# Moving one block's gate work behind the last transposes, and a 1/sqrt chain ahead of a put-off subtraction, in the z stage of an attention and gMLP kernel

## The chip, the cores and the metric

The kernel runs on one core of one Trainium2 chip. The metric is the device time of one execution in microseconds. Before the change it is 1726.86 us, the median of three runs (1726.46 to 1728.48).

## What is computed

Two pre-norm residual layers on `x` of 2048 x 512, in float32:

```
x = A_x
h  = x + attention(layernorm(x))            # 32 heads of 16, full softmax
# gMLP on layernorm(h):
z  = gelu(layernorm(h) @ w_in)              # 512 -> 2 x 688
z1 = z[:, :688]
z2 = layernorm(z[:, 688:])
g  = w_sp @ z2 + b_sp[:, None]              # mixes the 2048 rows
h2 = h + (z1 * g) @ w_out
```

Products that must be exact enough for float32 are made from two float16 parts of each factor (high part, and the difference "low part"), three matmuls each (`mm3`, lines 106 to 109).

## The kernel before, in words

The kernel has three large stages, each written out in an explicit order that the engines keep: attention (up to about 1294 us in the profile), the **z stage** (lines 1237 to 1280, from there to 1455 us), and the **final stage** (from line 1425 on), which multiplies by `w_sp` and `w_out`.

The z stage takes the 2048 rows in 16 blocks of 128, in the order `h_rows` = 0, 1, 8, 9, 2, 10, 3, 11, ..., 7, 15. Iteration `k` of its loop handles block `row[k]`; so iteration 12 is block 6, iteration 13 block 14, iteration 14 block 7 and iteration 15, the last, block 15. The work of an iteration, in the order of the code:

- `make_h` (740 to 752) for the block two iterations ahead (`new`): 12 matmuls on TensorE, then on VectorE the sum with `x` (749) and its statistics (752). The last two iterations have no `new`.
- `split_o` (731 to 738) for the block three ahead: ScalarE makes the high part (735), VectorE the low part (738).
- `make_z(sb, 1, 0)`: 12 matmuls and a gelu on ScalarE (1190) for the first half of the second part of z. `make_z(sb, 1, 1)`, `(0, 0)` and `(0, 1)` follow further down. The tile `z1` of a block is made by the first two, `z0` by the last two; `z0` has one buffer, `z1` four.
- `turn` (1170 to 1177) for the next block: four transposes on TensorE (1175) of the normalised `hn`, then ScalarE copies them out as float16 (`hT`, line 98) and VectorE makes the low part (104). The next iteration's matmuls need both. It stands behind the first `make_z`, in iteration 14 alone behind the second.
- the put-off difference: `subs.pop()(nc.vector)` makes the low part of one gate operand (`b21`, line 1195) that the iteration before left over. Blocks 8 to 14 leave one.
- the **1/sqrt chain of h**: `scale_h` (754 to 757, with `rstd_of`, 111 to 132) and `minus_mean` (764 to 767), ten small VectorE instructions from the variance of h to `nb`, the last input of `hn`.
- `bn_stats` of z on VectorE (1262).
- `hn` on ScalarE (1268), for the block two ahead; TensorE transposes it in the next iteration.
- `gate_z` (1203 to 1235), the **gate work**: a store of `z0` to device memory from ScalarE's queue (1207); VectorE's 1/sqrt chain of z (1209 on), ending in another `nb` (766); the normalisation on ScalarE (1212); and the operands of the final stage in `T`: sums and differences of quarters of z, each with a high part (1194) and a low part (1195), mostly on GpSimd (1218, 1228, 1231, 1234). A block under 8 gives `b11` and `t1`; a block from 8 on gives `t2`, `b22`, `t3`, `b21` and `n4`. The last block has some of these on VectorE and ScalarE.

Each engine executes its own instructions in the order of the code. The final stage begins on TensorE with `product(A, "b11")` (1445), which takes `b11` of the blocks 0 to 7 in turn, then `t1` (1454), `t2` (1463), `b22` (1465), `t3` (1470), `b21` (1475) and `n4` (1485); its weights `raw_w` come by DMA (1430, 1432) and are measured on VectorE (1322) before TensorE's matmul in `measure_w` (1328).

Of the kernel before, what the change touches and what calls it, by code (L numbers as in the profile page):

```python
# [27 lines left out]
NB = S // P  # L28
# [31 lines left out]
def block_kernel(ctx: ExitStack, tc: tile.TileContext, x, wqkv, wo, w_in, w_sp4, b_sp, w_out, out):  # L60
# [7 lines left out]
    nc = tc.nc  # L68
# [26 lines left out]
    def split(hi, lo, src, eh=None, el=None):  # L95

        if eh == "act":
            nc.scalar.activation(hi, src, AF.Copy)  # L98
        elif eh == "pool":
            nc.gpsimd.tensor_copy(hi, src)  # L100
        else:
            nc.vector.tensor_copy(hi, src)
        back = hi if hi.dtype == F16 else hi.bitcast(F32)
        (nc.gpsimd if el == "pool" else nc.vector).tensor_sub(lo, src, back)  # L104

    def mm3(ps, lh, ll, rh, rl, first, last, **kw):
        nc.tensor.matmul(ps, lh, rh, start=first, stop=False, **kw)  # L107
        nc.tensor.matmul(ps, lh, rl, start=False, stop=False, **kw)  # L108
        nc.tensor.matmul(ps, ll, rh, start=False, stop=last, **kw)  # L109

    def rstd_of(pool, var, n, between=lambda: None, up=1.0):

        hv = pool.tile([P, n], F32, name=f"rs_v{n}")
        nc.vector.tensor_scalar(hv, var, EPS, 0.5 / up ** 2, op0=ALU.add, op1=ALU.mult)
        r = pool.tile([P, n], F32, name=f"rs_r{n}")
        nc.vector.tensor_scalar(r.bitcast(I32), hv.bitcast(I32), -0.5, GUESS,
                                op0=ALU.mult, op1=ALU.add)
        t = pool.tile([P, n], F32, name=f"rs_t{n}")
        for i in range(3):
            if i == 1:  # L120
                between()

            if n == 1:
                nc.vector.tensor_scalar(t, r, r, hv, op0=ALU.mult, op1=ALU.mult)  # L124
                u = pool.tile([P, 1], F32, name="rs_u", bufs=6)
                nc.vector.tensor_scalar(u, t, 1.5, r, op0=ALU.subtract, op1=ALU.mult)  # L126
                r = u
            else:
                nc.vector.tensor_mul(t, r, r)
                nc.vector.tensor_mul(t, t, hv)  # L130
                nc.vector.scalar_tensor_tensor(r, t, 1.5, r, op0=ALU.subtract, op1=ALU.mult)
        return r
# [626 lines left out]
    def new_hn(sb):  # L759
        mv, rs = scale_h(sb)  # L760
        hns[sb] = e2.tile([P, D], F32, name="hn", bufs=3)
        nc.vector.tensor_scalar(hns[sb], xrs.pop(sb), mv[:, 0:1], rs, op0=ALU.subtract, op1=ALU.mult)

    def minus_mean(pool, mv, rs):
        nb = pool.tile([P, 1], F32, name="nb")
        nc.vector.tensor_scalar(nb, rs, mv[:, 0:1], -1.0, op0=ALU.mult, op1=ALU.mult)
        return nb
# [396 lines left out]
    with ExitStack() as mid:  # L1164
        m2 = mid.enter_context(tc.tile_pool(name="mid_2", bufs=2))
        zs, zst = {}, {}
        ps = mid.enter_context(tc.tile_pool(name="mid_ps", bufs=5, space=PSUM))
        pt = mid.enter_context(tc.tile_pool(name="mid_pt", bufs=2, space=PSUM))

        def turn(sb):  # L1170

            hn = hns.pop(sb)
            tp = pt.tile([P, DB, P], F32, name="tp")
            for d in range(DB):
                nc.tensor.transpose(tp[:, d, :], hn[:, d * P:(d + 1) * P], ident)
            hTs[sb] = [m2.tile([P, DB, P], F16, name=f"hT{i}") for i in range(2)]
            split(hTs[sb][0], hTs[sb][1], tp, "act")

        def new_z(sb):
            zs[sb] = [m2.tile([P, FH], F32, name=f"z{i}", bufs=1 + 3 * i) for i in range(2)]  # L1180
            zst[sb] = m2.tile([P, 2, 6], F32, name="zst")

        def make_z(sb, i, c):

            hT, f = hTs[sb], slice(i * FH + c * FC, i * FH + (c + 1) * FC)
            acc = ps.tile([P, 512], F32, name="acc")
            for d in range(DB):
                mm3(acc[:, :FC], hT[0][:, d, :], hT[1][:, d, :],
                    wi2[0][:, d, f], wi2[1][:, d, f], d == 0, d == DB - 1)
            nc.scalar.activation(zs[sb][i][:, c * FC:(c + 1) * FC], acc[:, :FC], AF.Gelu_apprx_tanh,  # L1190
                                 scale=gelu_down)

        def parts(name, k, src, eh, el):
            (nc.gpsimd.tensor_copy if eh == "pool" else nc.scalar.copy)(T[name][0][:, k, :], src)
            sub = lambda e: e.tensor_sub(T[name][1][:, k, :], src, T[name][0][:, k, :])
            if el == "later":
                subs.append(sub)
            else:
                sub(nc.gpsimd if el == "pool" else nc.vector)

        subs = []

        def gate_z(sb, meanwhile):

            z = zs.pop(sb)
            rows = slice(sb * P, (sb + 1) * P)
            nc.scalar.dma_start(z_scr[rows, :], z[0])
            mv = m2.tile([P, 2], F32, name="zmv")
            nc.vector.bn_aggr(mv, zst.pop(sb))
            rs = rstd_of(m2, mv[:, 1:2], 1, up=Z2_UP)  # L1210
            nb = minus_mean(m2, mv, rs)
            nc.scalar.activation(z[1], z[1], AF.Identity, bias=nb, scale=rs)
            zs[sb] = z[1]
            meanwhile()
            if sb < HB:
                b1, b2 = z[1][:, :FC], z[1][:, FC:]
                parts("b11", sb, b1, "act", "pool")
                nc.gpsimd.tensor_sub(b1, b2, b1)
                parts("t1", sb, b1, "pool", "pool")
                return  # L1220

            k = sb - HB
            (t1, b12), (b21, b22) = ((t[:, :FC], t[:, FC:]) for t in (zs.pop(k), zs.pop(sb)))
            last = k == HB - 1
            e = nc.vector if last else nc.gpsimd
            el, eh = (None, "act") if last else ("pool", "pool")
            t2 = m2.tile([P, FC], F32, name="t2", bufs=1)
            e.tensor_sub(t2, b22, t1)
            parts("t2", k, t2, eh, el)
            parts("b22", k, b22, "pool" if last else "act", "pool")  # L1230
            nc.gpsimd.tensor_sub(b12, b22, b12)
            parts("t3", k, b12, "pool", "pool")
            parts("b21", k, b21, "pool" if last else "act", "pool" if last else "later")
            nc.gpsimd.tensor_sub(t2, b21, t2)
            parts("n4", k, t2, "pool", "pool")

        row = dict(enumerate(h_rows))
        with tc.manual_schedule(engines={E.PE, E.Activation, E.DVE, E.Pool, E.SP}):
            asked.pop(0)()
            turn(row[0])  # L1240
            new_hn(row[1])
            for k in range(NB):
                sb, new = row[k], row.get(k + 2)
                if new is not None:
                    for _ in make_h(new, ps.tile([P, 512], F32, name="acc")):
                        pass
                if k + 3 < NB:
                    split_o(row[k + 3])
                new_z(sb)
                make_z(sb, 1, 0)  # L1250
                if k + 1 < NB and k != NB - 2:
                    turn(row[k + 1])
                if subs:
                    subs.pop()(nc.vector)
                if new is not None:
                    mv, rs = scale_h(new)
                    nb = minus_mean(e2, mv, rs)
                make_z(sb, 1, 1)
                if k == NB - 2:
                    turn(row[k + 1])  # L1260
                for c in range(2):
                    nc.vector.bn_stats(zst[sb][:, c, :], zs[sb][1][:, c * FC:(c + 1) * FC])
                make_z(sb, 0, 0)
                make_z(sb, 0, 1)
                hTs.pop(sb)
                if new is not None:
                    hns[new] = e2.tile([P, D], F32, name="hn", bufs=3)
                    nc.scalar.activation(hns[new], xrs.pop(new), AF.Identity, bias=nb, scale=rs)
                if k == 1:
                    invert()  # L1270
                if k >= NB - 8:
                    ask()

                def meanwhile():
                    if k + 4 < NB:
                        asked.pop(0)()
                    if k + 5 < NB:
                        asked.append(load_o(row[k + 5]))

                gate_z(sb, meanwhile)  # L1280
    early.close()
    late.close()

# [258 lines left out]
```

## Time and profile before

| what | value |
|---|---|
| median of three runs | 1726.86 us (1726.46 to 1728.48) |
| the profiled execution: its time, its span | 1726.86 us, 1725.1 us |
| busy share of the span | TensorE 99%, VectorE 83%, ScalarE 76%, GpSimd 47% |
| first transposes of the z stage, its last matmul | 1294.60 us, 1455.07 us |
| first matmul of the final stage | 1455.22 us |

PE is TensorE's matmuls, PEld its weight loads, DVE is VectorE, ACT ScalarE, POOL GpSimd, SP the DMA queue of SyncE, ACTq the one of ScalarE. A row of a timeline gives the start in us from the span's start, the duration, the engine and line, the operation with output and input, and in brackets how long the engine sat idle before it and what released it. Matmuls are pipelined: a row of 128x344 shows 0.31 us, though the next one starts 0.146 us later; so the distance of starts tells more than the brackets.

### The profile page before, as it was taken

How to read it: one execution, taken by the hardware profiler on the slowest of the kernel's cores; microseconds unless marked ns; L12 is line 12 of the kernel's file. 1: busy time of each engine (PE TensorE's matmuls, PEld its weight loads, DVE VectorE, ACT ScalarE, POOL GpSimd, SP SyncE). 2: the span in 40 equal slices, each digit the busy share in tenths (PEclk: the TensorE clock that was granted, in tenths of full speed). 3: DMA queues.
4: the chain of work that ended last, by engine and by line, in shares of the span. 5: the costliest groups of instructions: out<-in, count | busy, mean ns of one | idle time of the engine just before them, and what ended most of it. 6: DMA issues, size and time to landing. Idle time of an engine off the chain costs nothing.

```text
span 1725.1 us, 36747 instructions
## 1 busy us (share of the span) xinstructions
PE 1708.8 (99%) x13583; PEld 653.4 (38%) x13583; DVE 1438.4 (83%) x3030; ACT 1318.7 (76%) x2598; POOL 815.5 (47%) x1076
## 2 busy tenths in 40 slices
PE   9999999999999999999999999999999999999999
PEld 4433222222222222222222222222216566666665
DVE  7688999999999999999999999999927886433234
ACT  4334999999999999999999999999994554221111
POOL 1231867776672267687677866400013766110010
PEclk9999999999999999999999999999999999999999
DMA  5534332342231234344345343300124464654540
GB/s 183 162 97 144 101 88 69 100 98 81 75 71 27 60 105 117 113 149 135 103 121 146 115 147 103 80 20 12 45 51 135 136 184 159 228 179 145 170 139 25
DMA packets 183932, 190.51 MB, mean 110 GB/s; under 512 B 65704, under 2 KB 134632, under 8 KB 183752
## 3 DMA queue, kind: packets, MB, share of 16 engines
q1 hardware_dynamic: 181448, 182.53, 36.2%
q10 hardware_dynamic: 2304, 5.64, 0.8%
q8 instruction: 106, 1.74, 0.4%
q14 instruction: 74, 0.61, 0.1%
HBM read 122.10 MB, written 65.93 MB: 109 GB/s over the span
## 4 chain that ended last, share of the span: by engine, by line
PE 76%; DVE 15%; DMA 3%; ACT 2%; issue 2%; POOL 2%; SPq 1%; DVEq 0%; ACTq 0%; POOLq 0%
PE pv L828 26%; PE s L803 17%; PE m L223 9%; DVE mx L228 7%; PE acc L107 4%; PE g L109 4%; PE g L108 4%; PE g L107 4%; PE acc L109 3%; PE acc L108 3%; DVE ab L237 1%; DMA rc<-r_scr 1%; DVE og L838 1%; DVE rs_t L124 1%; DVE rs_u L126 1%
## 5 line engine op out<-in xcount | busy, mean ns | idle before, releaser
L812 ACT ACTIVATE pt<-s 128x512 f32<-128x512 f32 x1968 | 1006.3, 637 | 5.1 <-PE m L223 4.0
L228 DVE TENSOR_REDUCE mx<-m 128x1 f32<-128x512 f32 x1510 | 947.5, 682 | 12.6 <-PE m L223 3.9
L803 PE MATMUL s<-qst,kst 50*128 50x512 f16 x2048 | 604.3, 379 | 0.2
L828 PE MATMUL pv<-pt,vst 128*32 128x256 f32 (+1 forms) x6056 | 598.1, 466 | 4.1 <-DVE og L838 1.3
L223 PE MATMUL m<-kst,qst 48*128 48x512 f16 x1510 | 452.4, 381 | 0.0
L803 PEld LDWEIGHTS <-kst 50*128 50x128 f16 x2048 | 131.9, 94 | 352.1 <-issue 323.7
L828 PEld LDWEIGHTS pv<-pt,vst 128*32 128x32 f32 x6056 | 119.5, 108 | 290.3 <-issue 276.9
L223 PEld LDWEIGHTS <-qst 48*128 48x128 f16 x2048 | 159.2, 93 | 173.7 <-issue 124.3
L223 PE MATMUL m<-uvs,qst 48*128 48x512 f16 x504 | 190.5, 380 | 0.3 <-DVE mx L228 0.3
L245 POOL TENSOR_SCALAR nm<-nm 128x16 f32<-128x16 f32 x32 | 6.6, 206 | 359.7 <-DVE nm L242 359.7
L237 DVE CUSTOM_DVE_ANT_0 ab<-m,ab 128x512 f32<-128x512 f32 x252 | 170.5, 677 | 2.7 <-ACT ab L233 2.7
L233 ACT ACTIVATE ab<-m 128x512 f32<-128x512 f32 x252 | 157.3, 624 | 16.5 <-PE m L223 15.8
L989 POOL TENSOR_TENSOR op<-raw,op 128x512 f16<-128x512 f32 x80 | 92.9, 1161 | 6.0
L1467 POOL TENSOR_TENSOR pr<-pr,z 128x344 f32<-128x344 f32 x8 | 7.3, 912 | 176.9 <-DVE pr L1466 173.0
L912 POOL TENSOR_TENSOR raw<-raw 128x512 f32<-128x512 f32 (+1 forms) x84 | 83.3, 991 | 6.7
L917 POOL TENSOR_TENSOR acc_sp<-acc_sp,raw 128x512 f32<-128x512 f32 x63 | 80.5, 1277 | 4.5
L107 PE MATMUL acc<-wi,hT 128*128 128x344 f16 x256 | 79.1, 309 | 1.4 <-ACT hT L98 1.4
L1362 ACT ACTIVATE pr<-pr,up 128x304 f32<-128x304 f32 (+1 forms) x32 | 17.0, 574 | 81.9 <-DVE up L1316 81.9
L109 PE MATMUL acc<-wi,hT 128*128 128x344 f16 x256 | 79.1, 309 | 0.3 <-DVE hT L104 0.3
L108 PE MATMUL acc<-wi,hT 128*128 128x344 f16 x256 | 79.1, 309 | 0.0
L1408 DVE SCALAR_TENSOR_TENSOR h<-acc,low,h 128x512 f32<-128x512 f32 (+1 forms) x33 | 24.1, 732 | 45.8 <-PE acc L109 32.5
L909 POOL TENSOR_SCALAR raw<-raw 128x512 f32<-128x512 f32 (+1 forms) x88 | 52.3, 594 | 19.5 <-DMA raw<-in_wqkv 12.2
(240 smaller groups left out, 2280.1 us busy)
## 6 DMA issues: line engine op xcount, KB each, us to landing
raw<-in_w_sp SPq DMA_DIRECT2D x128, 256.0 KB
s_scr<-op SPq DMA_DIRECT2D x64, 256.0 KB
op<-s_scr SPq DMA_DIRECT2D x32, 512.0 KB
a_scr<-op SPq DMA_DIRECT2D x48, 256.0 KB
op<-a_scr SPq DMA_DIRECT2D x24, 512.0 KB
o_scr<-og SPq DMA_DIRECT2D x64, 128.0 KB
qst<-q_scr SPq DMA_DIRECT2D x192, 32.0 KB
kst<-k_scr SPq DMA_DIRECT2D x48, 128.0 KB
```

The lines of the kernel that those rows point to most:

```text
L107: nc.tensor.matmul(ps, lh, rh, start=first, stop=False, **kw)
L108: nc.tensor.matmul(ps, lh, rl, start=False, stop=False, **kw)
L109: nc.tensor.matmul(ps, ll, rh, start=False, stop=last, **kw)
L223: nc.tensor.matmul(acc, q[r, p, c], keys[r, p], start=True, stop=True)
L228: nc.vector.reduce_max(at(t, e if t else e - 1), acc, axis=AX.X)
L233: nc.scalar.activation(ab[0], acc, AF.Abs)
L237: nc.vector.tensor_tensor_reduce(ab[0], acc, ab[0], 0.5, LOW, ALU.add, ALU.max, at(0, 0))
L803: nc.tensor.matmul(s, kst[hg % 2][r, p, kb * P:(kb + 1) * P], qst[hg * NQ + qb][r, p, :], start=True, stop=True)
L812: nc.scalar.activation(pts[p, kb][:, t, :], s, AF.Exp, scale=scales_[hg // 2])
L828: nc.tensor.matmul(pv[0][32 * j:32 * j + 32, a:b], vst[hg % 2][:, c:c + 32], pts[j % 2, kb][:, j // 2, a:b], start=kb == 0, stop=kb == NB - 1,
L912: pool.tensor_mul(got[0] if n else acc, got[0], got[0])
L989: chores.append((lambda: pool.tensor_sub(t[0][:, 1], of(), t[0][:, 0]), TT))
```

## The change

It does two things in the loop of the z stage. The gate work of iteration 13 (block 14) isn't issued at the end of that iteration but held in `put_off`, and issued in iteration 14 behind `turn` of the last block. And in every iteration the 1/sqrt chain of h with its `minus_mean` stands ahead of the put-off difference, not behind it.

```diff
-        subs = []
+        subs, put_off = [], []
...
                 make_z(sb, 1, 0)
                 if k + 1 < NB and k != NB - 2:
                     turn(row[k + 1])
-                if subs:
-                    subs.pop()(nc.vector)
                 if new is not None:
                     mv, rs = scale_h(new)
                     nb = minus_mean(e2, mv, rs)
+                if subs:
+                    subs.pop()(nc.vector)
                 make_z(sb, 1, 1)
                 if k == NB - 2:
                     turn(row[k + 1])
+                    put_off.pop()()
...
-                def meanwhile():
+                def meanwhile(k=k):
...
-                gate_z(sb, meanwhile)
+                if k == NB - 3:
+                    put_off.append(lambda sb=sb, then=meanwhile: gate_z(sb, then))
+                else:
+                    gate_z(sb, meanwhile)
```

The number and kind of instructions stay the same. First place, VectorE in iteration 12 (`b21_1` is the low part of block 13's gate operand, `mv` and `nb` begin and end the chain of h, `zst` takes the statistics of z). Before, from the low part of `o` on:

```order
L738 SCALAR_TENSOR_TENSOR o21_22576<-o_22394,fig3_1844,o20_22575 128x512
L104 TENSOR_TENSOR hT1_22602<-tp_22596,hT0_22601 128x512
L1195 TENSOR_TENSOR b21_1_20667<-z1_22433,b21_0_20666 128x344
L756 BN_AGGR mv_22606<-st_22573 128x2
L114 TENSOR_SCALAR rs_v1_22608<-mv_22606 128x1
```

and now, the end of the same stretch:

```order
L126 TENSOR_SCALAR rs_u_22619<-rs_t1_22612,rs_u_22616 128x1
L766 TENSOR_SCALAR nb_22621<-rs_u_22619,mv_22605 128x1
L1195 TENSOR_TENSOR b21_1_20667<-z1_22433,b21_0_20666 128x344
L1263 BN_STATS zst_22581<-z1_22580 128x6 x2
L1209 BN_AGGR zmv_22673<-zst_22581 128x2
```

The difference has moved from ahead of the chain's ten instructions to behind them; it still stands ahead of the statistics of z. It is so in the six iterations 3, 4, 6, 8, 10 and 12. A seventh difference, block 14's, went in iteration 14 and now goes in iteration 15.

Second place, ScalarE from `hn` of the last block on (`z0_22714` and `z1_22715` are block 14's z, `z1_22840` and `z0_22839` block 7's, `hT0` the last block's transposes). Before:

```order
L1268 ACTIVATE hn_22802<-xr_22404,nb_22756,rs_u_22754 128x512
L1207 DMA z_scr_81<-z0_22714 128x688
L1212 ACTIVATE z1_22715<-z1_22715,nb_22823,rs_u_22821 128x688
L1194 CAST b22_0_20668<-z1_22715 128x344
L1194 CAST b21_0_20666<-z1_22715 128x344
L1190 ACTIVATE z1_22840<-acc_22842,fig0_1841 128x344
L1190 ACTIVATE z1_22840<-acc_22857,fig0_1841 128x344
L98 ACTIVATE hT0_22876<-tp_22871 128x512
L1190 ACTIVATE z0_22839<-acc_22882,fig0_1841 128x344
L1190 ACTIVATE z0_22839<-acc_22896,fig0_1841 128x344
```

and now (block 7's tiles are `z1_22807` and `z0_22806`):

```order
L1269 ACTIVATE hn_22802<-xr_22404,nb_22756,rs_u_22754 128x512
L1190 ACTIVATE z1_22807<-acc_22809,fig0_1841 128x344
L1190 ACTIVATE z1_22807<-acc_22823,fig0_1841 128x344
L98 ACTIVATE hT0_22842<-tp_22837 128x512
L1207 DMA z_scr_81<-z0_22714 128x688
L1212 ACTIVATE z1_22715<-z1_22715,nb_22863,rs_u_22861 128x688
L1194 CAST b22_0_20668<-z1_22715 128x344
L1194 CAST b21_0_20666<-z1_22715 128x344
L1190 ACTIVATE z0_22806<-acc_22881,fig0_1841 128x344
L1190 ACTIVATE z0_22806<-acc_22895,fig0_1841 128x344
```

Two gelus and the copy of the last transposes have passed the store, the normalisation and two casts of block 14.

Third place, VectorE at the same point. Before, the end of block 14's chain of z, its put-off difference, and then the low part of the last block's transposes:

```order
L126 TENSOR_SCALAR rs_u_22821<-rs_t1_22813,rs_u_22818 128x1
L766 TENSOR_SCALAR nb_22823<-rs_u_22821,zmv_22807 128x1
L1195 TENSOR_TENSOR b21_1_20667<-z1_22715,b21_0_20666 128x344
L104 TENSOR_TENSOR hT1_22877<-tp_22871,hT0_22876 128x512
L1262 BN_STATS zst_22841<-z1_22840 128x6 x2
```

and now:

```order
L766 TENSOR_SCALAR nb_22756<-rs_u_22754,mv_22740 128x1
L1263 BN_STATS zst_22716<-z1_22715 128x6 x2
L104 TENSOR_TENSOR hT1_22843<-tp_22837,hT0_22842 128x512
L1209 BN_AGGR zmv_22847<-zst_22716 128x2
L114 TENSOR_SCALAR rs_v1_22849<-zmv_22847 128x1
```

The low part `hT1` has passed block 14's whole chain of z and its put-off difference. GpSimd's order stays as it was; the inputs of its part of block 14's gate work come from ScalarE's normalisation, which now stands later.

## The prediction, made before the run

> **What bounds the kernel now.** I read the page first, then TensorE's waits within the z stage, then the timelines of the engines around those waits.
>
> ```profile
> span 1725.1 us, 36747 instructions
> PE 1708.8 (99%) x13583; PEld 653.4 (38%) x13583; DVE 1438.4 (83%) x3030; ACT 1318.7 (76%) x2598; POOL 815.5 (47%) x1076
> ```
>
> TensorE is the bound, so the change is worth what it takes from TensorE's idle time, and a part of it at most. The profiled execution took 1726.86 us, the median of the runs shown; a term found in its trace is subtracted from that time. About 0.2%, 3.5 us, is what a measurement of this kernel can tell from no change.
>
> In the z stage TensorE waits in two kinds of place. The first, TensorE at the start of iteration 15:
>
> ```profile
> 1446.07 0.31 PE L109 MATMUL acc<-wi,hT 128*128 128x344 f16 x1
> 1447.78 0.32 PE L107 MATMUL acc<-wi,hT 128*128 128x344 f16 x1 [1.40 <-ACT hT L98]
> 1447.93 0.31 PE L108 MATMUL acc<-wi,hT 128*128 128x344 f16 x1
> 1448.50 0.32 PE L109 MATMUL acc<-wi,hT 128*128 128x344 f16 x1 [0.26 <-DVE hT L104]
> ```
>
> Matmuls follow each other in 0.146 us. From 1446.07 to 1447.78 is 1.71, so 1.56 are lost; from 1447.93 to 1448.50 another 0.42. The sum is **1.99 us**: TensorE waits for the copies of the last block's transposes, which stand on ScalarE and VectorE behind block 14's gate work.
>
> The second kind is small and repeats: TensorE wants to transpose and `hn` isn't there yet. Its waits, and the turns of iterations 12 and 13:
>
> ```profile
> PE tp L1175 <- ACT hn L1268: 1.6, 5, 0.7
> ...
> 1422.62 0.60 PE L1175 MATMUL tp<-ident,hn 128*128 128x128 f32 x4
> 1423.05 0.31 PE L107 MATMUL acc<-wi,hT 128*128 128x344 f16 x1
> ...
> 1432.50 0.31 PE L109 MATMUL acc<-wi,hT 128*128 128x344 f16 x1
> 1433.03 0.66 PE L1175 MATMUL tp<-ident,hn 128*128 128x128 f32 x4 [0.23 <-ACT hn L1268]
> 1433.53 0.31 PE L107 MATMUL acc<-wi,hT 128*128 128x344 f16 x1
> ```
>
> The turn of iteration 13 starts 0.53 behind the last matmul, not 0.146, and its four transposes take 0.50 and not 0.43: 0.45 lost. The brackets hide 0.16 of each wait; with that added to the 1.6 us, a sixth wait hidden wholly, and 0.07 for slow transposes, the six come to about 2.9 us. They stand in iterations 4, 5, 7, 9, 11 and 13, each behind an iteration with a put-off difference.
>
> **What sets `hn`.** ScalarE over two iterations, and VectorE in iteration 12:
>
> ```profile
> 1415.06 0.96 ACT L1212 ACTIVATE z<-z,nb,rs_u 128x688 f32<-128x688 f32 x1 [2.58 <-DVE nb L766]
> ...
> 1421.22 0.81 ACT L1268 ACTIVATE hn<-xr,nb,rs_u 128x512 f32<-128x512 f32 x1 [1.83 <-DVE nb L766]
> ...
> 1424.61 0.96 ACT L1212 ACTIVATE z<-z,nb,rs_u 128x688 f32<-128x688 f32 x1 [2.58 <-DVE nb L766]
> ...
> 1432.17 0.81 ACT L1268 ACTIVATE hn<-xr,nb,rs_u 128x512 f32<-128x512 f32 x1 [2.85 <-DVE nb L766]
> ...
> 1435.56 0.96 ACT L1212 ACTIVATE z<-z,nb,rs_u 128x688 f32<-128x688 f32 x1 [2.58 <-DVE nb L766]
> ```
>
> ```profile
> 1427.12 0.75 DVE L738 SCALAR_TENSOR_TENSOR o<-o,fig,o 128x512 f16<-128x512 f32 x1 [1.16 <-ACT o L735]
> ...
> 1428.04 0.69 DVE L104 TENSOR_TENSOR hT<-tp,hT 128x512 f16<-128x512 f32 x1 [0.16 <-ACT hT L98]
> 1428.65 1.09 DVE L1195 TENSOR_TENSOR b<-z,b 128x344 f16<-128x344 f32 x1
> 1429.66 0.17 DVE L756 BATCH_NORM_AGGREGATE mv<-st 128x2 f32<-128x6 f32 x1
> ...
> 1432.05 0.93 DVE L1262 BATCH_NORM_STATS2 zst<-z 128x6 f32<-128x344 f32 x2
> ```
>
> VectorE and ScalarE form a closed loop: ScalarE's normalisation (1212) waits for VectorE's `nb`, the high part of `o` (735) stands behind it, VectorE's low part (738) waits for that, and from line 104 on VectorE runs without a gap to the next `nb`. Two turns of this loop take 1435.56 - 1415.06 = 20.50 us. TensorE needs less: from the turn at 1422.62 to that at 1433.03 are 10.41, less the 0.39 lost ahead of it 10.02, or 20.04 for two. **So the small waits come from a slower loop, not from where the chain stands in it.** The difference stays ahead of the statistics (1262), hence in the loop.
>
> **Part 1: the chain of h ahead of the difference (six iterations).** The chain starts at 1428.65 and not 1429.66, so `hn` is 1.01 us earlier in these iterations. In the others it doesn't move: there `hn` ends at 1421.22 + 0.81 = 1422.03 and TensorE takes it at 1422.62. Since a waiting transpose starts about 0.05 behind its `hn` (1432.98 to 1433.03), that is 0.54 of slack. TensorE can gain on the loop only until it eats this: the waits move to the even iterations 6 to 12. By iteration 13 TensorE is about 0.95 us ahead of before. Then two more rows cap it:
>
> ```profile
> 1437.37 0.59 ACT L98 ACTIVATE hT<-tp 128x512 f16<-128x512 f32 x1
> ...
> 1441.11 0.81 ACT L1268 ACTIVATE hn<-xr,nb,rs_u 128x512 f32<-128x512 f32 x1 [1.58 <-DVE nb L766]
> ...
> 1444.50 0.96 ACT L1212 ACTIVATE z<-z,nb,rs_u 128x688 f32<-128x688 f32 x1 [2.58 <-DVE nb L766]
> ```
>
> ```profile
> 1437.99 0.69 DVE L104 TENSOR_TENSOR hT<-tp,hT 128x512 f16<-128x512 f32 x1 [1.09 <-ACT hT L98]
> ...
> 1441.95 0.21 DVE L1209 BATCH_NORM_AGGREGATE zmv<-zst 128x2 f32<-128x12 f32 x1
> ```
>
> ```profile
> 1439.07 0.31 PE L109 MATMUL acc<-wi,hT 128*128 128x344 f16 x1
> ...
> 1442.28 0.60 PE L1175 MATMUL tp<-ident,hn 128*128 128x128 f32 x4
> ```
>
> Iteration 14 has no `make_h`, so TensorE reaches its `hT` at once. The low part is there at 1438.68, which lets the matmul of 1439.07 start at 1438.73, 0.34 earlier; the last `hn` ends at 1441.92, which lets the turn of 1442.28 start at 1441.97, 0.31 earlier. So part 1 is worth **0.3 us** if the loop keeps its pace.
>
> The pace hangs on GpSimd. What ran there beside the difference:
>
> ```profile
> 1428.53 0.83 POOL L1195 TENSOR_TENSOR b<-z,b 128x344 f16<-128x344 f32 x1
> 1429.33 1.18 POOL L1231 TENSOR_TENSOR z<-z,z 128x344 f32<-128x344 f32 x1
> ...
> 1431.13 0.84 POOL L1195 TENSOR_TENSOR t<-z,t 128x344 f16<-128x344 f32 x1
> ...
> 1448.90 0.91 POOL L1231 TENSOR_TENSOR z<-z,z 128x344 f32<-128x344 f32 x1
> ```
>
> ```profile
> 1446.38 0.52 DVE L1195 TENSOR_TENSOR b<-z,b 128x344 f16<-128x344 f32 x1 [1.92 <-ACT b L1194]
> ```
>
> Six of the seven differences take 1.09 and the seventh 0.52: in the six, a GpSimd instruction that began 0.12 earlier (1428.53) runs, the difference ends 0.38 behind its end (1429.36 to 1429.74), and GpSimd's next one takes 1.18 and not 0.91. In its new place the difference starts 1428.65 + 1432.05 - 1429.66 = 1431.04. GpSimd's subtraction of 1431.13 comes 0.27 earlier, as nothing lengthens line 1231 any more: 1430.86. It is under way again, ends at 1431.70, and lets the difference end at 1432.08, against 1432.13 if the old 1.09 were simply moved. So the loop gains 0.05 or 0.06 in each of six iterations, 0.35 at most, and part 1 lies between 0.3 and 0.65. I take 0.5, the middle.
>
> The Trainium skill ("SBUF — State Buffer", section "Who interferes with whom") says that a VectorE instruction with two SBUF inputs and a GpSimd instruction that reads SBUF block each other, and that whichever issues first keeps the other out for its whole length. The 0.52 against 1.09 agrees. By this rule the margin of 0.18 us between GpSimd's start and VectorE's decides: 0.5 for part 1 as above, or the first rival's sum.
>
> **Part 2: block 14's gate work behind the last turn.** With that turn at 1441.97 the copies follow it on engines that are free but for two gelus, and `hT` is complete near 1444.1 (0.66 for the transposes, 0.59 and 0.69 for the copies, with two short steps between). TensorE wants it at 1445.90. The 1.99 us go whole. What is moved is late instead. VectorE's chain of z starts at 1444.04 and not 1441.95, **2.09 later**, and with it the normalisation (1446.59 instead of 1444.50) and GpSimd's part:
>
> ```profile
> 1445.54 0.92 POOL L1228 TENSOR_TENSOR t<-z,z 128x344 f32<-128x344 f32 x1 [5.14 <-ACT z L1212]
> ...
> 1453.54 0.84 POOL L1195 TENSOR_TENSOR b<-z,b 128x344 f16<-128x344 f32 x1
> ```
>
> ```profile
> 1458.43 0.31 PE L108 MATMUL g<-b,op 128*128 128x344 f16 x1
> ```
>
> GpSimd works without a gap from 1445.54 through block 14's part to the low part of block 7's `b11` at 1453.54. Moved by 2.09 this ends at 1456.47. TensorE wants it in the eighth group of the first product, at 1458.43 before, now 1.99 + 0.31 earlier: 1456.13. **A new wait of 0.4 us** (0.34 and a start of 0.05). The next product wants `t1` 24 matmuls or 3.5 us behind that, and GpSimd has `t1` about 2.5 us behind `b11`, so that is covered.
>
> The store of `z0` moves too, and block 7's gelus into the one buffer wait for it:
>
> ```profile
> 1359.80 4.57 DMA z_scr<-z
> ```
>
> Issued near 1443.4, a store of 4.6 us (the chain of waits) has landed at 1448.0; ScalarE gets to the gelu at 1448.4. Block 7's own store goes near 1449.3 and makes ScalarE wait at the last block's `z0`, with only the last normalisation behind it, whose `nb` comes later still. Cost: nothing, as long as a store lands within 5 us. Block 14's `b21` goes to VectorE's iteration 15; the sixth product wants it, over 15 us later. `meanwhile` issues nothing in iteration 13. Behind GpSimd's run stand the memset of the last sixth of `raw_w` and SyncE's two small loads into it, 2.1 later:
>
> ```profile
> 1456.76 0.53 POOL L1429 MEMSET raw_w<- 128x512 f32 x1
> ```
>
> ```profile
> 1463.57 3.65 DVE L1322 TENSOR_REDUCE w<-raw_w 128x1 f32<-128x512 f32 x6 [3.29 <-DMA raw_w<-in_w_out]
> ```
>
> VectorE reads that sixth last, near 1466.5, over 6 us behind the new memset; the other five leave at TensorE's last z matmul and come earlier with it. Cost nothing.
>
> **The sum.** -1.99 - 0.5 + 0.4 = -2.1 us: 1726.86 - 2.1 = **1724.8**. With 0.3 to 0.65 for part 1 and 0.2 to 0.8 for the new wait it is 1724.4 to 1725.4.
>
> **Rivals.** *The difference meets a free port* (12%): if it starts ahead of GpSimd's subtraction it takes 0.52, six iterations are 0.5 shorter, the loop is faster than TensorE and all 2.9 us go: -1.99 - 2.9 + 0.4 = -4.5, 1722.4. Against it stands the 0.18 us by which GpSimd is first, the same in each of six repeats.
>
> *GpSimd holds the tail* (9%): VectorE's seventh difference now falls into GpSimd's run, and each meeting adds 0.27. With more of them, or GpSimd starting later, the wait at `b11` grows one for one; at 2.5 us nothing is left: up to 1726.9.
>
> *GpSimd's queue goes first* (5%): if in the new place the next GpSimd instruction too (line 1234, 0.92) gets ahead of the waiting difference, each of six iterations grows by about 0.9, `hn` of the last turn comes 5.4 later (1447.3, against 1442.28 before, so TensorE loses 5.1), and the time is 1726.86 + 5.1 - 1.99 + 0.4 = 1730.4, slower. It decides from the second instruction on; before, VectorE got in behind the first, six times of six.
>
> *The move shows nothing* (3%): a wait that I don't see takes the 2 us; 1726.9.
>
> **How the numbers follow.** The forecast has 71%. Faster by over 0.2% is the first rival, 0.12; slower the third and a little more, 0.06; the rest is 0.82. The range runs from the first rival, 1722.3, to the second, 1726.9, which leaves the third out.
>
> **What would show it.** No wait at line 107 for `hT` at the start of the last iteration; a wait of about 0.4 at the end of the first product for line 1195 on GpSimd; waits of about 0.4 for `hn` in iterations 6, 8, 10 and 12 instead of 7 to 13; differences of still about 1.05 us. Six differences of 0.52 would make the first rival right; 1.9 the third.

## The result, and the profile after

The changed kernel takes **1724.36 us**, the median of 19 runs (1723.85 to 1725.05); the kernel before 1726.76, the median of 19 (1725.97 to 1728.48). The ratio is 0.9986, 95% interval 0.998 to 0.9993: 2.4 us faster, which is within 0.2%. The profiled execution took 1723.98 us, 2.88 less than the one of before. Page of the changed kernel:

```profile
span 1722.2 us, 36747 instructions
...
PE 1709.8 (99%) x13583; PEld 653.6 (38%) x13583; DVE 1438.1 (84%) x3030; ACT 1318.6 (77%) x2598; POOL 813.6 (47%) x1076
```

TensorE's waits in the z stage and the first product now, and those of its weight loads. A column each: total us, times, longest.

```profile
PE acc L109 <- DVE hT L104: 0.3, 1, 0.3
```

```profile
PEld L745 <- DVE o L738: 1.7, 4, 0.5
PEld tp L1175 <- ACT hn L1269: 1.3, 5, 0.3
PEld L109 <- DVE hT L104: 0.6, 1, 0.6
PEld L109 <- issue: 0.3, 1, 0.3
PEld L107 <- ACT hT L98: 0.3, 1, 0.3
```

The wait of the transposes on `hn` (line 1175, 1.6 us before) and the one on ScalarE's `hT` (line 107, 1.4) are gone from TensorE's list. Its weight loads still show small ones, with a new kind, line 745: the product by `wo` waits for the low part of `o` (738), an output of the same loop. TensorE's timeline at the three places of the forecast, the start of iteration 14, the last turn with the start of iteration 15, and the eighth group of the first product:

```profile
1436.88 0.31 PE L109 MATMUL acc<-wi,hT 128*128 128x344 f16 x1
1437.12 0.32 PE L107 MATMUL acc<-wi,hT 128*128 128x344 f16 x1
1437.28 0.31 PE L108 MATMUL acc<-wi,hT 128*128 128x344 f16 x1
1437.85 0.32 PE L109 MATMUL acc<-wi,hT 128*128 128x344 f16 x1 [0.26 <-DVE hT L104]
...
1441.08 0.66 PE L1175 MATMUL tp<-ident,hn 128*128 128x128 f32 x4
...
1444.92 0.31 PE L109 MATMUL acc<-wi,hT 128*128 128x344 f16 x1
1445.07 0.31 PE L107 MATMUL acc<-wi,hT 128*128 128x344 f16 x1
...
1455.13 0.31 PE L107 MATMUL g<-b,op 128*128 128x344 f16 x1
1455.52 0.31 PE L108 MATMUL g<-b,op 128*128 128x344 f16 x1
```

From 1444.92 to 1445.07 is the plain distance of 0.146: the 1.99 us at the start of iteration 15 are gone whole. At the start of iteration 14 there is a new loss of 0.09 + 0.42 = 0.52 for `hT`, and in the eighth group one of 0.24, since GpSimd's low part of `b11` (1454.63, 0.84 long) ends at 1455.47. It is the last of GpSimd's run behind block 14's normalisation, which starts with the first row:

```profile
1446.60 0.92 POOL L1228 TENSOR_TENSOR t<-z,z 128x344 f32<-128x344 f32 x1 [7.11 <-ACT z L1212]
...
1454.63 0.84 POOL L1195 TENSOR_TENSOR b<-z,b 128x344 f16<-128x344 f32 x1
```

I added up in each trace what TensorE's distances of starts have above the plain ones, from the first z matmul to the end of the first product. In all nine kernels of this study the profiled time is the first z matmul plus that sum plus 423.9 (423.84 to 424.00), so this table is the whole of what differs between them:

| kernel | first z matmul | for `hn` and `o`, iterations up to 13 | start and turn of iteration 14 | start of 15 | `b11` | sum | profiled time |
|---|---|---|---|---|---|---|---|
| before | 1298.06 | 2.93 | 0 | 1.99 | 0 | 4.92 | 1726.86 |
| after | 1298.12 | 1.07 | 0.57 | 0 | 0.24 | 1.88 | 1723.98 |
| chain only | 1299.12 | 0.65 | 0.57 | 2.23 | 0 | 3.45 | 1726.53 |
| put-off only | 1297.89 | 2.38 | 0 | 0 | 0.23 | 2.61 | 1724.35 |
| difference behind z | 1298.03 | 0 | 0 | 0 | 0.23 | 0.23 | 1722.11 |
| difference twice | 1298.67 | 7.35 | 1.71 | 0 | 0.51 | 9.58 | 1732.25 |
| store later | 1298.40 | 0 | 0 | 0.92 | 0 | 0.92 | 1723.21 |
| difference behind z alone | 1297.65 | 0 | 0 | 0 | 0 | 0 | 1721.49 |
| `b11` on VectorE | 1297.92 | 1.59 | 0.57 | 0 | 0 | 2.17 | 1724.03 |

The first column differs by 1.5 us though no kernel differs there: in these nine executions the attention stage ended that unevenly, which can be one part of the spread of the runs.

**The pace of the loop.** ScalarE's normalisation of z, one iteration in two, in the changed kernel:

```profile
1393.81 0.96 ACT L1212 ACTIVATE z<-z,nb,rs_u 128x688 f32<-128x688 f32 x1 [3.53 <-DVE nb L766]
...
1414.23 0.96 ACT L1212 ACTIVATE z<-z,nb,rs_u 128x688 f32<-128x688 f32 x1 [3.52 <-DVE nb L766]
...
1434.66 0.96 ACT L1212 ACTIVATE z<-z,nb,rs_u 128x688 f32<-128x688 f32 x1 [3.52 <-DVE nb L766]
```

Two turns take 20.42 us, 0.08 less than before and still more than TensorE's 20.04. VectorE and GpSimd around the difference in its new place:

```profile
1430.07 0.21 DVE L766 TENSOR_SCALAR nb<-rs_u,mv 128x1 f32<-128x1 f32 x1
1430.20 1.03 DVE L1195 TENSOR_TENSOR b<-z,b 128x344 f16<-128x344 f32 x1
1431.16 0.93 DVE L1263 BATCH_NORM_STATS2 zst<-z 128x6 f32<-128x344 f32 x2
```

```profile
1430.02 0.84 POOL L1195 TENSOR_TENSOR t<-z,t 128x344 f16<-128x344 f32 x1
1430.82 1.21 POOL L1234 TENSOR_TENSOR t<-z,t 128x344 f32<-128x344 f32 x1
```

GpSimd is first by 0.18 us, as the prediction worked out, and the difference takes 1.03, six times of six (1.01 to 1.03).

**Where the loop starts.** The normalisation in iteration 2, before and after, with the store ahead of it:

```profile
1331.31 0.33 ACTq L1207 DMA_DIRECT2D z_scr<-z  x1
1331.68 0.96 ACT L1212 ACTIVATE z<-z,nb,rs_u 128x688 f32<-128x688 f32 x1 [4.69 <-DMA o<-o_scr]
```

```profile
1330.82 0.36 ACTq L1207 DMA_DIRECT2D z_scr<-z  x1
1331.23 0.96 ACT L1212 ACTIVATE z<-z,nb,rs_u 128x688 f32<-128x688 f32 x1 [4.17 <-DMA o<-o_scr]
```

VectorE's `nb` for it, in the kernel before:

```profile
1328.19 0.21 DVE L766 TENSOR_SCALAR nb<-rs_u,zmv 128x1 f32<-128x1 f32 x1
```

It was there at 1328.4. The 3.3 us up to the normalisation are spent on the store: it waits for a load of `o` that SyncE issued from 1323.97 on:

```profile
1323.97 2.81 SPq L721 DMA_DIRECT2D o<-o_scr  x4
```

The order of the code is the same in both kernels here; the 0.45 between them is how late that load landed. Over the eight traces in which the store stands there, the normalisation starts at 1330.82 to 1332.36.

So the 2.9 us between the two profiles are: 0.45 this start of the loop, 0.44 the loop itself (from iteration 2 to 12 its normalisations lie 103.87 us apart before and 103.43 after, 0.07 for each of six differences), 0.3 the slack at the last turn (before, `hn` ended at 1441.92 and the turn started at 1442.28), 1.99 the start of iteration 15, less 0.24 for `b11`. Without the 0.45, which is none of the change's, 2.5, beside 2.4 between the medians.

### The profile page after: what moved, and what is told of

Same layout as the page of the kernel before. It is cut to its first block, busy times and chain, and to the rows that moved or that the text cites. A ratio compares the mean times of both kernels' runs of the same rounds, so it can differ in the third digit from the quotient of the medians.

```text
span 1722.2 us, 36747 instructions
## 1 busy us (share of the span) xinstructions
PE 1709.8 (99%) x13583; PEld 653.6 (38%) x13583; DVE 1438.1 (84%) x3030; ACT 1318.6 (77%) x2598; POOL 813.6 (47%) x1076
## 4 chain that ended last, share of the span: by engine, by line
PE 74%; DVE 14%; DMA 4%; POOL 3%; ACT 2%; SPq 2%; issue 2%; ACTq 0%; DVEq 0%; POOLq 0%
PE pv L828 25%; PE s L803 17%; PE m L223 9%; DVE mx L228 7%; PE g L109 3%; PE g L108 3%; PE g L107 3%; PE acc L107 3%; PE acc L109 3%; PE acc L108 3%; DMA rc<-r_scr 2%; DVE ab L237 1%; DVE og L838 1%; DMA raw<-in_w_sp 1%; DVE rs_t L124 1%
```

## The experiments

My theory after the result: one loop, VectorE's two chains with the difference and ScalarE between them, sets all of TensorE's waits by its length and by its start. Rivals: the waits for `hn` come from where the chain of h stands; the two parts are independent; or other waits take over.

**One part alone.** The first kernel has only the chain of h ahead of the difference:

```diff
-                if subs:
-                    subs.pop()(nc.vector)
                 if new is not None:
                     mv, rs = scale_h(new)
                     nb = minus_mean(e2, mv, rs)
+                if subs:
+                    subs.pop()(nc.vector)
```

> Only the chain of h stands ahead of the put-off difference; block 14's gate work stays at the end of iteration 13. My theory: the loop of VectorE and ScalarE is the pace up to the last block's copies, and each of six differences takes 1.02 us and not 1.09 (rows of the changed kernel), so the loop gains 0.4 to 0.6 us and the start of iteration 15, which hangs on ScalarE behind block 14's normalisation, moves by just that: about 0.5 us below the kernel before, TensorE's two waits for hT at that start still there and together 2 us or more. Rival (the chain's place makes hn earlier and TensorE gains all of its small waits): 1.3 us or more below. Rival (part 1 does nothing): no change.

Measured: 1726.53 us against 1726.57, ratio 1.0002 (0.9993 to 1.0011). The 1.3 of the first rival is outside; between 0.5 and nothing the times can't tell. The trace can: the differences take 1.02 to 1.03, and the normalisations of iterations 2 and 12 lie 103.50 apart, 0.37 less than before. TensorE loses less up to iteration 13 (0.65) but more at the start of 15:

```profile
1445.48 0.31 PE L109 MATMUL acc<-wi,hT 128*128 128x344 f16 x1
1447.43 0.32 PE L107 MATMUL acc<-wi,hT 128*128 128x344 f16 x1 [1.65 <-ACT hT L98]
```

1.81 here, and 0.42 at the low part. What TensorE gains ahead it waits for there, since that `hT` hangs on ScalarE in the loop. In the table its sum is 1.47 below that of the kernel before, but its first z matmul came 1.06 later; the loop sets the end, and 0.41 is left. So by the trace part 1 alone is worth the loop's own 0.4 us, which the times don't show.

The second has only the put-off:

```diff
...
                 if k == NB - 2:
                     turn(row[k + 1])
+                    put_off.pop()()
...
+                if k == NB - 3:
+                    put_off.append(lambda sb=sb, then=meanwhile: gate_z(sb, then))
+                else:
+                    gate_z(sb, meanwhile)
```

> Only block 14's gate work is put off; the difference stays ahead of the chain of h. My theory: 1.99 us of waits for hT go, a wait of 0.24 for GpSimd's low part of b11 comes (both lie at a fixed distance from the last turn), the small waits for hn stay in iterations 5 to 13 as before: 1.75 us below the kernel before. Then the two parts alone give 0.5 + 1.75 = 2.25 and the changed kernel, at 2.4, has a little over the sum, since in it the last turn starts as soon as hn is there. Rival (the whole gain of the change is the put-off): 2.4 below, equal to the changed kernel.

Measured: 1724.81 against 1726.57, 1.76 less, ratio 0.999 (0.9981 to 0.9999). In the trace the start of iteration 15 has no wait, `b11` costs 0.23, the waits for `hn` stand in iterations 5, 7, 9, 11 and 13 and the differences take 1.09. Part 2 is 1.75 us, as expected. The times alone can't tell this from the rival's 2.4; that the 2.38 for `hn` and `o` stay in the trace speaks against the rival. With 0.4 for part 1 alone the two make 2.15; the changed kernel's 2.4 to 2.5 has the 0.3 of slack at the last turn on top, which only counts once nothing waits behind that turn. This too is read from the traces; no difference of times here shows 0.3.

**The difference out of the loop.** As the changed kernel, with:

```diff
-                if subs:
-                    subs.pop()(nc.vector)
                 make_z(sb, 1, 1)
...
             nb = minus_mean(m2, mv, rs)
+            if subs:
+                subs.pop()(nc.vector)
             nc.scalar.activation(z[1], z[1], AF.Identity, bias=nb, scale=rs)
```

> As the changed kernel, but the put-off difference stands behind the chain of z too, outside the loop that sets hn. My theory (this loop, lengthened by the difference, is the pace): the loop is 1 us shorter in each of six iterations, quicker than TensorE's 20.04 us for two, so the waits left in the changed kernel at the turns of iterations 8, 10 and 12, at the products by wo there (together 1.1 us) and most of the 0.5 at the start of iteration 14 go: 1.1 to 1.6 below the changed kernel, 3.5 to 4.0 below the kernel before. Rival (hn is set by something other than the loop with the difference in it, or VectorE has no room behind the chain of z and hands the delay on by lines 749 and 738): within 0.3 of the changed kernel.

Measured: 1722.37 against 1726.57, 4.2 less, ratio 0.9977 (0.9968 to 0.9986). That is just over the 3.5 to 4.0 expected, which I had counted from the changed kernel's profile, an execution 0.38 below its median. TensorE's list of waits is empty between 1300 and 1460 us; 0.23 for `b11` is all that its distances show. In the new place, behind `nb` of z:

```profile
1408.99 1.20 DVE L1195 TENSOR_TENSOR b<-z,b 128x344 f16<-128x344 f32 x1
1410.10 0.74 DVE L749 SCALAR_TENSOR_TENSOR xr<-acc,fig,xr 128x512 f32<-128x512 f32 x1
```

```profile
1408.54 1.27 POOL L729 TENSOR_TENSOR o<-o,rc 128x512 f32<-128x512 f32 x1
```

The difference even takes longer here, 1.20, as it meets GpSimd's product of `o` and `rc` (729); that costs nothing, since ScalarE has its `nb` already.

The opposite, each difference issued twice in the place that it has in the changed kernel:

```diff
                 if subs:
+                    subs[-1](nc.vector)
                     subs.pop()(nc.vector)
```

> As the changed kernel, with each put-off difference issued twice in its place (the same values written again). My theory: in six iterations the second one stands in the loop, so each adds its time: 0.5 us if it runs at once, 1.2 if GpSimd's next instruction (line 1234) goes ahead of it and holds it off. That is 3.0 to 7.2 us above the changed kernel, with waits for hn in every second iteration. Rival (the loop has room): no change, or under 1 us.

Measured: 1732.13 against 1726.57, ratio 1.0031 (1.0019 to 1.0043); 7.8 above the changed kernel's median. ScalarE's normalisation, VectorE's pair and GpSimd's row beside it:

```profile
1399.56 0.96 ACT L1212 ACTIVATE z<-z,nb,rs_u 128x688 f32<-128x688 f32 x1 [4.68 <-DVE nb L766]
...
1421.12 0.96 ACT L1212 ACTIVATE z<-z,nb,rs_u 128x688 f32<-128x688 f32 x1 [4.66 <-DVE nb L766]
```

```profile
1415.53 2.17 DVE L1195 TENSOR_TENSOR b<-z,b 128x344 f16<-128x344 f32 x2
```

```profile
1415.35 0.83 POOL L1195 TENSOR_TENSOR t<-z,t 128x344 f16<-128x344 f32 x1
1416.14 1.19 POOL L1234 TENSOR_TENSOR t<-z,t 128x344 f32<-128x344 f32 x1
```

Two turns take 21.56 us and not 20.42: 1.14 for each second difference, 6.9 in six. Of the 7.7 that the table has over the changed kernel the rest is 0.27 at `b11` and a later start of the loop (1332.36). So the 7.8 lies over the 3.0 to 7.2 expected; of the two prices expected for one difference, 0.5 and 1.2, the 1.14 is near the upper one, because the second one waits for GpSimd's line 1234, as the first one does for 1195. It got in behind that one instruction each time: the two go by turns, and GpSimd's queue never went first twice. The Trainium skill ("SBUF — State Buffer", section "Who interferes with whom") says that a VectorE instruction with two SBUF inputs contends with a GpSimd instruction that reads SBUF, and that whichever issues first keeps the other out for its whole length; the 1.11 to 1.13 of the second differences agree. Where both engines had work waiting, VectorE was next, each time.

**The start of the loop.** As the kernel before, with two stores issued an iteration later:

```diff
...
-            nc.scalar.dma_start(z_scr[rows, :], z[0])
+            store = lambda: nc.scalar.dma_start(z_scr[rows, :], z[0])
+            if sb in (h_rows[0], h_rows[2]):
+                stores.append(store)
+            else:
+                store()
...
                     split_o(row[k + 3])
+                if stores:
+                    stores.pop()()
```

> As the kernel before, without either part of the change; only the stores of z0 of the first and third block are issued one iteration later, behind line 735 on ScalarE. In the traces so far ScalarE's normalisation in iteration 2 starts 3 to 4 us behind its nb, because the store ahead of it waits for a load of o that SyncE issued (4.17 us of idle time in the changed kernel). My theory: the loop is the pace for the rest of the stage, so how late it starts counts as much as how long it is; with the store out of its way it starts iteration 3 about 3.5 us earlier, TensorE's small waits for hn (2.9 us) go, and the wait at the start of iteration 15 shrinks by the rest: 3.0 to 3.7 us below the kernel before. Rival (the loop would wait for the loads of o all the same, or catches up by itself within an iteration or two): no change.

Measured: 1722.83 against 1726.67, 3.8 less, ratio 0.9978 (0.9969 to 0.9987), just over what was expected, with the slow loop, the old order and no put-off. ScalarE in iteration 2 and 3, and TensorE at the start of iteration 15:

```profile
1328.03 0.96 ACT L1216 ACTIVATE z<-z,nb,rs_u 128x688 f32<-128x688 f32 x1 [0.69 <-DVE nb L766]
1329.27 0.33 ACTq L1207 DMA_DIRECT2D z_scr<-z  x1
...
1335.18 0.55 ACT L1190 ACTIVATE z<-acc,fig 128x344 f32<-128x344 f32 x1 [2.02 <-DMA z_scr<-z]
```

```profile
1443.47 0.31 PE L109 MATMUL acc<-wi,hT 128*128 128x344 f16 x1
1444.11 0.32 PE L107 MATMUL acc<-wi,hT 128*128 128x344 f16 x1 [0.33 <-ACT hT L98]
```

The normalisation starts at 1328.03, 3.65 earlier than before, and is held by its `nb` alone. A gelu now waits 2.02 for the late store, and nothing comes of it. The loop still loses 0.46 in two iterations on TensorE, but from a lead: no wait up to the last turn, and 0.92 left at the start of iteration 15.

**The difference behind z, and nothing else.** The kernel before with the one move of the third experiment:

> As the kernel before, with the put-off difference behind the chain of z and nothing else: no gate work is put off, and the chain of h needn't pass the difference. My theory: the 1.99 us at the start of iteration 15 too come from the loop's lag. With a loop quicker than TensorE, block 14's normalisation is done before the last turn, its copies find ScalarE and VectorE free, and GpSimd reaches block 7's b11 before TensorE asks for it, so that the put-off is worth nothing and its new wait of 0.23 is not there: 4.2 to 4.8 us below the kernel before, as fast as the kernel with both (4.2) or 0.2 faster. Rival (the put-off is needed by itself): at least 1.5 us slower than the kernel with both, 2.7 below the kernel before or less.

Measured: 1722.12 us against 1726.67, **4.55 less**, ratio 0.9975 (0.9964 to 0.9985), the fastest kernel here. ScalarE in iteration 14:

```profile
1437.88 0.96 ACT L1214 ACTIVATE z<-z,nb,rs_u 128x688 f32<-128x688 f32 x1 [1.00 <-DVE nb L766]
1438.87 0.86 ACT L1194 CAST b<-z 128x344 f16<-128x344 f32 x2
1439.63 0.98 ACT L1190 ACTIVATE z<-acc,fig 128x344 f32<-128x344 f32 x2
1440.51 0.59 ACT L98 ACTIVATE hT<-tp 128x512 f16<-128x512 f32 x1
```

```profile
1442.72 0.31 PE L109 MATMUL acc<-wi,hT 128*128 128x344 f16 x1
1442.87 0.31 PE L107 MATMUL acc<-wi,hT 128*128 128x344 f16 x1
```

The gate work of block 14 stands ahead of the copies as before, but the normalisation starts at 1437.88 and not 1444.50, and the copy is made in time. TensorE loses nothing at all, at `b11` neither. The put-off treats a symptom: with the loop quicker than TensorE it is worth nothing. Against the kernel with both, 4.2 below, the times can't tell the 0.35 apart; the 0.23 of `b11` is in the traces.

**The new wait.** As the changed kernel, with the last low part of `b11` on VectorE:

```diff
-                parts("b11", sb, b1, "act", "pool")
+                parts("b11", sb, b1, "act", None if sb == HB - 1 else "pool")
```

> As the changed kernel, with the low part of block 7's b11 on VectorE and not on GpSimd. My theory of the new wait at the end of the first product (0.24 us): GpSimd's queue, moved by the put-off, holds that low part. On VectorE it is done by about 1451, 4 us before TensorE asks, so the 0.24 goes and nothing takes its place: 0.2 below the changed kernel, less than the times can tell, so the trace decides. Rival (the wait is for something else, such as the weights' transfer or the bank of g): the 0.24 stays in the trace.

Measured: 1723.87 against 1726.67, ratio 0.9985 (0.9976 to 0.9994). In the trace the eighth group runs without a gap, so the 0.24 was GpSimd's queue:

```profile
1455.45 0.31 PE L107 MATMUL g<-b,op 128*128 128x344 f16 x1
1455.60 0.31 PE L108 MATMUL g<-b,op 128*128 128x344 f16 x1
```

The change's own 2.4 and this kernel's 2.8 can't be told apart by the times.

## Why the prediction was right, and where it was off

The forecast was 1724.8 us, and the medians gave 1724.36. That lies within the whole range and 0.04 under the 1724.4 that the sum's own terms allow. The two misses below point the same way, by 0.24 and 0.16, so the forecast isn't right by errors that cancel.

**The start of iteration 15, -1.99:** right, the whole of it, shown by the put-off alone.

**The wait for `b11`, +0.4:** right in kind and place, 0.24 in size. Both ends hang on the last turn, TensorE's wish and GpSimd's run. The step that put VectorE's chain of z 2.07 behind that turn (1441.97 to 1444.04) was 0.13 too long: it is 1443.02 after 1441.08, 1.94.

**Part 1, -0.5 (0.3 to 0.65):** the mechanism was right, the size not. The difference still meets GpSimd, and the loop stays the pace. It gained 0.07 by each difference and not 0.05 or 0.06, 0.44 in all and not 0.35 at most; the step "I take 0.5, the middle" then took half of the loop's gain, where the slack of 0.3 and the whole gain add: 0.74. In the profile another 0.45 came with the load on which the loop's start hangs, which the prediction never looked at.

**Where the waits would stand:** half right. Iterations 8, 10 and 12 have them, 6 doesn't. They are split in two, 0.18 at the product by `wo` and 0.12 at the transposes with 0.055 for slow ones, since `o` comes from the same loop. The cap in iteration 14 showed as the 0.52 for `hT`.

**The covers at zero** held: the table's constant of 423.9 leaves no room for a new wait behind the first product.

**The rivals:** the free port didn't come (1.03, not 0.52), nor did GpSimd's queue go first. GpSimd didn't hold the tail: its run up to the low part of `b11` takes 8.87 us (1446.60 to 1455.47) and took 8.84 before. The first rival's thought, that a loop faster than TensorE takes all of its waits away, was right: with the difference out of the loop the kernel is 4.55 faster. That its 4.5 is so near is partly chance, since the rival's sum holds a wait of 0.4 at `b11` and the 4.55 none; with the put-off the like kernel is 4.2 faster.

**What the reading missed:** it held the small waits and the 1.99 us for two kinds. They are one: the loop is 3.3 us late from iteration 2 and loses 0.46 in two iterations, and TensorE runs into it at `hn` and at the last `hT` alike. Either cure, a shorter loop or an earlier start, takes away most of both.

## What to carry to other kernels

When one engine waits a little in every second turn and a lot at the end, follow the loop that feeds it and compare its period with the engine's own; then move what doesn't feed the loop behind the last instruction that does, even where it takes longer. Moving such work to another place within the loop gains only what it saves in its own duration. Look for the first turn too: a late start is carried along by a slow loop to the end.

## What the runs showed of the hardware that wasn't expected

- A store issued by ScalarE held that engine for about 3.3 us after its data and the next instruction's inputs were there, until a load of SyncE landed. In the semaphore events of the trace of before, the store waits for the completion counter that this load raises, for the last time at 1330.94, and raises the same counter itself; the transfers of the two engines in the z stage share eight such counters. That store and the first block's, issued an iteration later, were worth 3.8 us.
- VectorE's difference takes 0.50 to 0.52 us alone, 1.01 to 1.13 behind GpSimd's instructions of 0.83 to 1.21, and 1.18 to 1.22 behind one of 1.27. GpSimd's subtraction of line 1231 or 1234, where it comes next, takes 1.18 to 1.21 and not 0.91 or 0.92. In each of the 48 meetings within the loop, in seven kernels, VectorE came right behind the instruction under way.
